# GpSimd instructions on the shared port also wait for the VectorE work that the plan puts ahead of them

## The chip, the cores and the metric

One core of one Trainium2 chip runs the whole kernel as one program. The metric is the device time of one execution in microseconds (us), and the time of a kernel is the median of several executions. The engines are TensorE (PE in the profile; its weight loads are PEld), VectorE (DVE), ScalarE (ACT), GpSimd (POOL) and SyncE (SP), which here only issues DMAs.

## What is computed

The input x has 2048 rows of 576 numbers. Its layernorm `xn` goes into two branches, and their results are added to x:

```
xn = (x - mean) / sqrt(var + 1e-5)                        # per row
A  = irfft2(rfft2(xn) * (w_r + 1j * w_i))                 # over rows and columns
q  = einsum("nd,dhc->nhc", xn, w_q)                       # 32 heads, 2 x 128 each
i1 = argmax(q[..., :128] @ k1.T);  i2 = argmax(q[..., 128:] @ k2.T)   # 8 keys each
e  = 8 * i1 + i2                                          # one of 64 experts
B  = sum over heads of gelu(xn . u[e]) * v[e]
out = x + A + B
```

The softmax of the reference runs over one candidate, so its weight is 1.

## The kernel before, in words

**How the work is tiled.** x is held as 16 tiles of 128 rows. For each tile `ln` (line 688) takes the row statistics, mostly on VectorE (`bn_stats`), for tiles 7, 9, 11, 13 and 15 on ScalarE. `folds` (line 742) adds and subtracts x and its mirror image along the columns: two instructions over 289 columns (tile `t` in the profile), then three over 145 to 288 columns (tile `A`). The sets `DE`, `DS`, `DF` and `DV` (lines 737 to 739) say which of them go to VectorE and which to GpSimd. `dft128` (line 759) is the first matmul of the Fourier transform. Meanwhile `fold_part` (line 851) folds the query weights with the keys, so that the scores become one matmul with x later; its weights are loaded by 32 DMAs.

Then 16 groups g of frequencies pass through `d_fwd`, `s_fwd`, `s_mul`, `s_inv` (lines 1017 to 1099). `s_mul` multiplies by W on VectorE (tiles `t1` and `t2`, from PSUM), combines the parts on GpSimd (`y`, two instructions of 128x289), lets ScalarE round to 16 bits (`yh`), GpSimd take the rest (`yh` again, 128x578) and ScalarE copy a part (`yl`). `s_inv` reads `yh` and `yl` on TensorE. Between the groups run eight blocks r of the expert branch: `x_t` (line 920) splits x into two 16-bit parts (GpSimd: `xT<-xf,xT`, 128x640), `scores` (line 938) does the matmuls, the gelu (ScalarE) and the maximum over keys (`mx<-banks`), and `route` and `combine` (lines 964 and 984) turn the winning keys into codes with VectorE instructions on 16-bit tiles (`w<-w,wt`, `w<-w,MT`, `w<-MT,iv`). `w_scale` (line 831) finds the scale of the next weights W: a maximum over partitions by a transpose on TensorE, `mxr` on VectorE and a matmul `banks<-id,mxr` on TensorE (`allmax`, line 667). Last, for 16 tiles t, `d_inv` and `fin` (lines 1105 and 1133) transform back, add the expert branch and write out.

**What sets the order.** The program is not issued as it is traced. Every call is recorded by `_Engine` as an op of `_Plan` (line 295) with an engine, a modelled cost, its dependences and a mark `port`. The mark (line 348) is set for each GpSimd instruction that has an input, and for a VectorE instruction whose output is in SBUF and that has two or more SBUF inputs, or is a copy or `tensor_scalar` with one. `forward` (line 409) walks through time: each engine takes, of the ops that can start, the one of the best rank in the hand-kept list `RANK`; an op with the mark `port` can't start before the last op with the mark has ended, on either engine. It returns the order and each op's planned start. `issue` (line 522) then issues all ops in the order of their planned starts, under `manual_schedule`, so each engine executes its own ops in exactly this order; waits between the engines come only from data (what an op reads, or the buffer it overwrites). All recorded calls are issued at line 540, which is why the profile names L540 everywhere.

So the plan's rule that two ops with the mark don't overlap is a rule of the plan alone: the issued program does not hold an engine back for it.

Of the kernel before, what the change touches and what calls it, by code (L numbers as in the profile page):

```python
# [294 lines left out]
class _Plan:  # L295
# [223 lines left out]
                    stale.add(ops[k].eng)  # L519
        return max(free.values()), order, slot, start  # L520

    def issue(self):

        self.prepare()
        ops = self.ops
        self.tiles = sorted({v for o in ops for v in o.tiles}, key=lambda v: v.order)
        for o in ops:
            o.held = []
            o.opens = sorted(o.tiles, key=lambda v: v.order) if o.eng == "tensor" else []
            o.after = [(k, self.latency(o, ops[k])) for k in o.succ]  # L530
        for i, o in enumerate(ops):
            for j in o.pre:
                ops[j].held.append(i)
        _, order, slot, start = self.forward([-r for r in RANK])
        self.order = [(start[i], i) for i in order]
        for v, k in slot.items():
            v.slot = k
        for i in order:
            for fn, args, kw in ops[i].calls:
                fn(*[x.place() if isinstance(x, _Ps) else x for x in args],  # L540
                   **{k: x.place() if isinstance(x, _Ps) else x for k, x in kw.items()})


def body(tc, nc, a, out):
    with ExitStack() as ctx:
        ctx.enter_context(tc.manual_schedule())
        plan = _Plan(nc)
        _body(ctx, tc, nc, plan, a, out)
        plan.issue()


def _body(ctx, tc, nc, plan, a, out):
# [716 lines left out]
```

## Time and profile before

| | |
|---|---|
| median of 3 runs | 222.05 us (221.85 to 222.1) |
| the profiled execution's own time | 222.02 us |
| its span, first to last instruction | 220.1 us |
| mean granted TensorE clock | 0.992 |
| busy: PE, DVE, ACT, POOL | 194.9, 187.4, 130.5, 115.0 us |
| instructions: PE, DVE, ACT, POOL | 2324, 457, 308, 153 |
| DMA | 48.12 MB, mean 219 GB/s |

The span is split into stages by time: rows of the windows view give each engine's busy time within a stretch. A row of the timeline gives start, duration, engine, operation and tiles, and in brackets how long the engine stood idle before it and what released it. An instruction that has begun and is then held up shows no idle time: its row is longer than others of its shape. `banks` is PSUM.

### The profile page before, as it was taken

The numbers are of one execution on the slowest core, as the hardware profiler recorded it, in microseconds if no ns is written. First come the engines' busy times: TensorE is split into PE (matmuls) and PEld (weight loads), VectorE is DVE, ScalarE is ACT, GpSimd is POOL, SyncE is SP. The second block draws the span as 40 slices with busy tenths as digits, with TensorE's granted clock in tenths as the row PEclk, the third lists the DMA queues.
The fourth block names the chain that finished last, engine by engine and source line by source line (L and its number), as shares of the span: only waits on it lengthen the run. The fifth ranks groups of instructions, "written<-read, shape, count | busy, mean of one in ns | idle before, by whom it ended". The sixth has DMA issues, their size and how long they took to land.

```text
span 220.1 us, 6024 instructions
## 1 busy us (share of the span) xinstructions
PE 194.9 (89%) x2324; PEld 131.4 (60%) x2324; DVE 187.4 (85%) x457; ACT 130.5 (59%) x308; POOL 115.0 (52%) x153
## 2 busy tenths in 40 slices
PE   0179978989899999999999999969989999999990
PEld 0168557667656775657467465446555568877860
DVE  1999999971784967874899999999999999999980
ACT  2267989898857895849627934955635532213320
POOL 4644653602509840673416634867737239568760
PEclk9999999999999999999999999999999999999996
DMA  6999999999999999998224260201000000575466
GB/s 206 394 429 416 331 416 348 312 360 362 389 415 344 420 409 418 418 442 311 91 81 123 103 190 0 60 3 42 33 3 1 0 4 0 134 183 121 114 153 165
DMA packets 17020, 48.12 MB, mean 219 GB/s; under 512 B 2144, under 2 KB 8544, under 8 KB 16224
## 3 DMA queue, kind: packets, MB, share of 16 engines
q1 hardware_dynamic: 16992, 47.74, 61.1%
q8 instruction: 18, 0.29, 0.5%
q14 instruction: 10, 0.08, 0.1%
HBM read 43.01 MB, written 4.72 MB: 217 GB/s over the span
## 4 chain that ended last, share of the span: by engine, by line
PE 57%; DVE 29%; ACT 4%; issue 3%; DMA 3%; POOL 0%; ACTq 0%; DVEq 0%
PE banks L540 57%; DVE t L540 6%; DVE w L540 4%; DVE MT L540 4%; DVE A L540 3%; DVE st L540 2%; DVE rr L540 2%; DVE ABL L540 2%; DMA XN<-in_x_dram 2%; DVE AB L540 1%; ACT xT L540 1%; DMA w<-in_wq_dram 1%; DVE mx L540 1%; ACT xf L540 1%; DVE mm__96 L540 1%
## 5 line engine op out<-in xcount | busy, mean ns | idle before, releaser
L540 PE MATMUL banks<-MU,xT 128*128 128x512 f16 x192 | 45.7, 379 | 0.0
L540 PE MATMUL banks<-c,AB 128*128 128x145 f16 (+2 forms) x320 | 37.8, 252 | 0.0
L540 POOL TENSOR_TENSOR A<-t 128x287 f32<-128x287 f32 (+2 forms) x42 | 29.5, 722 | 15.6 <-DVE t L540 10.3
L540 POOL TENSOR_TENSOR y<-t,t 128x289 f32<-128x289 f32 x32 | 23.2, 748 | 22.7 <-DVE t L540 22.1
L540 PEld LDWEIGHTS <-xT 128*128 128x128 f16 x224 | 20.7, 98 | 23.2 <-issue 0.9
L540 DVE SCALAR_TENSOR_TENSOR t<-banks,wx,Wt 128x578 f32<-128x578 f32 x32 | 24.2, 810 | 3.9 <-PE banks L540 3.7
L540 POOL TENSOR_TENSOR yh<-y,yh 128x578 f16<-128x578 f32 x16 | 22.8, 1436 | 8.4 <-ACT yh L540 6.7
L540 PE MATMUL banks<-Rs,yl 128*99 128x128 f32 x64 | 12.0, 321 | 14.3 <-ACT Rs L540 11.8
L540 POOL TENSOR_TENSOR xT<-xf,xT 128x640 f16<-128x640 f32 x10 | 14.0, 1402 | 14.5 <-ACT xf L540 13.5
L540 ACT ACTIVATE AB<-banks 128x512 f32<-128x512 f32 (+1 forms) x32 | 18.8, 591 | 2.1 <-PE banks L540 1.8
L540 PEld LDWEIGHTS banks<-Rs,yl 128*99 128x99 f32 x64 | 8.6, 186 | 19.0 <-ACT Rs L540 14.2
L540 PE MATMUL banks<-w,KP 128*32 128x288 f32 x256 | 19.7, 414 | 0.1
L540 ACT ACTIVATE yh<-banks 128x290 f32<-128x290 f32 (+1 forms) x16 | 7.3, 458 | 20.8 <-PE banks L540 20.7
L540 PE MATMUL banks<-c,ABL 99*128 99x289 f16 (+1 forms) x64 | 18.8, 298 | 0.4 <-DVE ABL L540 0.4
L540 PEld LDWEIGHTS banks<-c,AB 128*128 128x128 f32 x128 | 17.9, 190 | 1.2 <-issue 0.5
L540 PE MATMUL banks<-Rs,A 128*128 128x128 f32 x128 | 18.5, 299 | 0.0
L540 DVE TENSOR_REDUCE MT<-w 128x128 bf16<-128x896 bf16 (+1 forms) x16 | 18.1, 1136 | 0.0
L540 PE MATMUL banks<-A,s 64*64 64x289 f32 x256 | 18.0, 411 | 0.0
L540 PEld LDWEIGHTS banks<-Rs,A 128*128 128x128 f32 x128 | 17.4, 214 | 0.9 <-issue 0.9
L540 PEld LDWEIGHTS <-AB 128*128 128x128 f16 x192 | 17.2, 147 | 0.1
L540 ACT ACTIVATE xT<-xf,bx 128x640 f16<-128x640 f32 x16 | 13.0, 821 | 5.6 <-PE banks L540 5.5
L540 POOL TENSOR_TENSOR t<-XN 128x289 f32<-128x289 f32 x14 | 11.9, 864 | 8.4 <-DVE A L540 4.2
(127 smaller groups left out, 417.8 us busy)
## 6 DMA issues: line engine op xcount, KB each, us to landing
w<-in_wq_dram SPq DMA_DIRECT2D x32, 576.0 KB, 6.8
xf<-in_xT_dram SPq DMA_DIRECT2D x16, 320.0 KB, 5.6
Wt<-in_W_dram SPq DMA_DIRECT2D x8, 578.0 KB, 6.7
out_dram<-XN SPq DMA_DIRECT2D x32, 144.0 KB, 2.5
XN<-in_x_dram SPq DMA_DIRECT2D x3, 1154.0 KB, 10.7
s<-in_s_dram SPq DMA_DIRECT2D x16, 192.0 KB, 5.1
XN<-in_xd_dram SPq DMA_DIRECT2D x2, 1152.0 KB, 9.7
XN<-in_xd_dram SPq DMA_DIRECT2D x1, 2304.0 KB, 12.3
```

The source lines that it names most:

```text
L540: fn(*[x.place() if isinstance(x, _Ps) else x for x in args], **{k: x.place() if isinstance(x, _Ps) else x for k, x in kw.items()})
```

## The change

While issuing, the new `issue` keeps a list of the VectorE instructions issued so far, each with its planned end plus 225 ns. For each GpSimd op with the mark `port` it looks up the last VectorE instruction on that list whose time is not later than the op's planned start plus 30 ns, that is, one planned to end at least 195 ns before the GpSimd op starts. If that is another one than for the last such op, the GpSimd instruction gets a dependence on it (`add_manual_dep`), which becomes a wait on VectorE's semaphore. No instruction is added to VectorE or taken from it, the order on every engine and the arithmetic stay, and VectorE gets no new wait.

```diff
-    def issue(self):
+    def issue(self, tc):
...
+        sync = mybir.DependencyInfo(mybir.DependencyClass.Sync, mybir.DependencyReason.DATA)
+        queue, held = [], None
         for i in order:
-            for fn, args, kw in ops[i].calls:
-                fn(*[x.place() if isinstance(x, _Ps) else x for x in args],
-                   **{k: x.place() if isinstance(x, _Ps) else x for k, x in kw.items()})
+            o = ops[i]
+            for fn, args, kw in o.calls:
+                ins = fn(*[x.place() if isinstance(x, _Ps) else x for x in args],
+                         **{k: x.place() if isinstance(x, _Ps) else x for k, x in kw.items()}).ins
+            if o.eng == "vector":
+                queue.append((start[i] + o.cost + 225, ins))
+            elif o.eng == "gpsimd" and o.port:
+                first = [v for t, v in queue if t <= start[i] + 30]
+                if first and first[-1] is not held:
+                    held = first[-1]
+                    tc.add_manual_dep(ins, held.name, sync, reason="port")
...
-        plan.issue()
+        plan.issue(tc)
```

Of the 149 GpSimd instructions of the plan, 143 carry the mark. The plan of the kernel before already holds all starts, so the partner of each can be read off it: 129 of them get a wait.

## The prediction

> **What bounds the kernel now.** I read the page first, then the windows view cut into stages, the waits of TensorE, and the timelines of single stretches. The windows show who is full in which stage (columns: stretch, its length, busy time of PE, PEld, DVE, ACT and POOL, granted clock, DMA share, GB/s).
>
> ```profile
> 4.60:43.00 38.40, 28.73 (x231) 22.58 (x232) 38.07 (x155) 28.01 (x83) 21.35 (x34) 1.00 0.98 381
> 60.00:87.00 27.00, 27.00 (x408) 17.30 (x408) 19.94 (x51) 20.11 (x40) 12.51 (x13) 1.00 1.03 400
> 137.00:145.00 8.00, 6.27 (x38) 3.12 (x36) 7.75 (x8) 6.49 (x12) 6.93 (x8) 1.00 0.15 41
> ```
>
> Until 43 us VectorE is the bound (38.07 of 38.40 us). From 60 to 87 us TensorE is full and so is the DMA. From 137 to 145 us VectorE is nearly full (7.75 of 8.00) while TensorE loses 1.73. GpSimd is the bound in none of them: even from 137 to 145 us it has 1.07 of 8 us free. So time can be won only where TensorE waits for VectorE, and before 43 us. From 113 to 176 us TensorE's waits are these, in total, times, longest:
>
> ```profile
> PE banks L540 <- DVE mxr L540: 2.2, 2, 1.9
> PE banks L540 <- DVE w L540: 0.5, 1, 0.5
> PE banks L540 <- DVE ABL L540: 0.4, 1, 0.4
> PE banks L540 <- ACT MT L540: 0.2, 1, 0.2
> ```
>
> These 3.3 us are the most that the stretch after 113 us can give back. The question is whether VectorE loses them to GpSimd. Here is VectorE's timeline around the longest of these waits, then GpSimd's, then TensorE's:
>
> ```profile
> 139.53 1.82 DVE L540 TENSOR_TENSOR w<-w,wt 128x896 bf16<-128x896 bf16 x1
> 141.28 1.50 DVE L540 TENSOR_TENSOR w<-w,MT 128x512 bf16<-128x512 bf16 x1
> 142.70 2.20 DVE L540 TENSOR_REDUCE MT<-w 128x128 bf16<-128x896 bf16 x2
> 144.82 0.27 DVE L540 TENSOR_REDUCE mxr<-banks 1x1 bf16<-1x128 f32 x1
> ...
> 146.32 1.09 DVE L540 TENSOR_REDUCE mx<-banks 128x128 f32<-128x896 f32 x1
> 147.32 0.42 DVE L540 TENSOR_TENSOR w<-w,MT 128x512 bf16<-128x512 bf16 x1
> ```
> ```profile
> 139.46 1.41 POOL L540 TENSOR_TENSOR xT<-xf,xT 128x640 f16<-128x640 f32 x1
> 140.82 1.68 POOL L540 TENSOR_TENSOR yh<-y,yh 128x578 f16<-128x578 f32 x1
> 143.57 1.40 POOL L540 TENSOR_TENSOR xT<-xf,xT 128x640 f16<-128x640 f32 x1 [1.07 <-ACT xf L540]
> 144.92 2.19 POOL L540 TENSOR_TENSOR yh<-y,yh 128x578 f16<-128x578 f32 x1
> ```
> ```profile
> 142.25 1.03 PE L540 MATMUL banks<-MU,xT 128*128 128x512 f16 x4
> 145.15 0.18 PE L540 MATMUL banks<-id,mxr 128*128 128x1 f16 x1 [1.88 <-DVE mxr L540]
> ```
>
> The second `w` instruction takes 1.50 us, and 0.42 at 147.32. The first takes 1.82; the same shape took 0.60 in this row:
>
> ```profile
> 130.25 0.60 DVE L540 TENSOR_TENSOR w<-w,wt 128x896 bf16<-128x896 bf16 x1
> ```
>
> Each of the two began just after a GpSimd instruction and ended when that one did, plus its own time. VectorE loses 1.22 + 1.08 = 2.3 us here, its queue brings `mxr` 2.3 us late, and TensorE stands for 1.88.
>
> By the Trainium skill, page "SBUF — State Buffer", section "Who interferes with whom", a VectorE instruction with two SBUF inputs and a GpSimd instruction that reads SBUF exclude each other for a whole instruction. These rows agree. The same section says that issue order alone decides who blocks; taken alone this speaks against the change, since an order then only passes the stall to the other engine. By it the sum below is kept only where GpSimd is off the path.
>
> **The change part by part.** Order, work and VectorE's queue stay. What is added is 129 waits in GpSimd's queue. Which VectorE instruction each waits for follows from the planned starts; all times below are from the trace. Laid on the trace, 48 of the partners end after the GpSimd instruction now starts: most between 7 and 42 us, some around 117 to 127, four around 139 to 147 (by 1.9 to 2.95 us: 141.35 against 139.46, 143.8 against 140.82), and a handful after. The other 81 waits are already met and cost nothing visible; a wait that was met late costs 0.08 us (GpSimd's 10.18 below, against VectorE's end at 9.16 + 0.94 = 10.10).
>
> *Stage 139 to 147.* The first `xT` will wait for the `w` at 139.53, the first `yh` for the first of the two reductions at 142.70, the second `xT` for a small `MT` instruction at 145.42, the second `yh` for the `mx` at 146.32. So both `w` run free, VectorE reaches `mxr` about 2.3 us earlier, and TensorE's 1.88 us go. What is late next is TensorE's own work, which ends at 143.28, so no more than 1.88. Behind the waiting instructions stands GpSimd's queue: `xT` to about 141.5 (held once more by the second `w`), `yh` to 142.8, `xT` to 145.1, `yh` to 146.8 on the new clock, which is 2.2 us ahead by then. The reader of the last is ScalarE:
>
> ```profile
> 148.99 0.52 ACT L540 ACTIVATE yl<-yh 128x396 f16<-128x396 f16 x1
> ```
>
> It will want `yh` at 148.99 - 2.2 = 146.8: just met. I take -1.9, between 0 and -1.9.
>
> *Stage 121 to 125.* The same on a smaller scale:
>
> ```profile
> 121.80 1.50 DVE L540 TENSOR_TENSOR w<-w,MT 128x512 bf16<-128x512 bf16 x1
> ...
> 125.03 0.73 DVE L540 TENSOR_TENSOR w<-w,MT 128x512 bf16<-128x512 bf16 x1
> ```
> ```profile
> 120.45 2.58 POOL L540 TENSOR_TENSOR yh<-y,yh 128x578 f16<-128x578 f32 x2
> ```
>
> VectorE gets 1.1 + 0.3 us back, but TensorE waited only 2.2 - 1.9 = 0.3 for it: -0.3.
>
> *Stage 157 to 163.* VectorE, GpSimd, TensorE:
>
> ```profile
> 157.78 0.14 DVE L540 TENSOR_SCALAR wx<-banks 128x2 f32<-128x2 f32 x1
> 157.85 0.27 DVE L540 TENSOR_TENSOR MT<-MT,fm 128x128 int32<-128x128 int32 x1
> 158.04 1.27 DVE L540 TENSOR_TENSOR al<-wx,mk 128x16 f32<-128x16 f32 x1
> ```
> ```profile
> 157.72 1.57 POOL L540 TENSOR_TENSOR yh<-y,yh 128x578 f16<-128x578 f32 x1 [0.80 <-ACT yh L540]
> ```
> ```profile
> 161.91 0.21 PE L540 MATMUL banks<-s,yh 64*128 64x128 f16 x1 [0.49 <-DVE w L540]
> ```
>
> `al` is sixteen columns and takes 1.27 us because `yh` is ahead of it. `yh` will wait for `wx` at 157.78, so it starts at 157.92 + 0.08 = 158.00, before `al` at 158.04. That is a race. GpSimd's 14.61 below shows who wins such a one: it starts 0.09 us before VectorE's `A` at 14.70, yet `A` takes its usual 0.44 and GpSimd's instruction 0.83 instead of the 0.44 of 10.18. I take VectorE to win: 1.1 us for VectorE, of which TensorE's 0.49 count, and the 0.2 of the list above, which is the wait for `MT` right behind it: 0.7. Bounds +0.3 (`yh` first, from a later start) and -0.7.
>
> *Stage 163 to 176.* TensorE's last wait of the list (0.4) ends a stretch in which VectorE lost 0.5 us to `y` additions that will now wait: -0.3, between 0 and -0.4.
>
> *Until 43 us.* VectorE is held in three places, the first two under a `t<-XN` of GpSimd quoted below, the third under one of the same kind:
>
> ```profile
> 9.16 0.94 DVE L540 TENSOR_TENSOR t<-XN 128x289 f32<-128x289 f32 x1
> ...
> 14.09 0.44 DVE L540 TENSOR_TENSOR t<-XN 128x289 f32<-128x289 f32 x1
> ...
> 14.70 0.44 DVE L540 TENSOR_TENSOR A<-t 128x288 f32<-128x288 f32 x1
> ...
> 21.92 0.91 DVE L540 TENSOR_TENSOR t<-XN 128x289 f32<-128x289 f32 x1
> ...
> 40.63 1.52 DVE L540 TENSOR_TENSOR A<-t 128x288 f32<-128x288 f32 x2
> ```
> ```profile
> 8.65 1.13 POOL L540 TENSOR_TENSOR t<-XN 128x289 f32<-128x289 f32 x1
> 10.18 0.44 POOL L540 TENSOR_TENSOR A<-t 128x145 f32<-128x145 f32 x1 [0.40 <-DVE t L540]
> ...
> 14.61 0.83 POOL L540 TENSOR_TENSOR A<-t 128x145 f32<-128x145 f32 x1 [0.45 <-DVE t L540]
> ...
> 21.83 1.67 POOL L540 TENSOR_TENSOR t<-XN 128x289 f32<-128x289 f32 x2
> ```
>
> Against 0.44 that is 0.50, 0.47 and about 0.8 (two instructions, 0.44 + 0.3): 1.8 us. The waits hold each of these GpSimd instructions behind the VectorE one. Their results are read 1.3 us or more later, mostly, which covers GpSimd's delay; where it doesn't, VectorE waits for the fold instead. But the gain must pass the stage from 60 to 87 us, where TensorE and the DMA are both full: it arrives only as far as the loads come earlier too. I take half, -0.9, between +0.3 and -1.8.
>
> *What the waits cost.* In the last stage GpSimd's additions run back to back, close ahead of TensorE:
>
> ```profile
> 200.58 2.70 POOL L540 TENSOR_TENSOR A<-t 128x289 f32<-128x289 f32 x4 [0.72 <-DVE t L540]
> 202.05 0.71 PE L540 MATMUL banks<-A,c 64*64 64x288 f32 x8
> ```
>
> The matmul starts 0.1 us after the second addition is over (200.58 + 2 x 0.675 = 201.93). Partners there end 0.3 us before the additions start, so I take 0.4 us of new waiting in all, between 0 and 1.1 (0.07 for each of 16 tiles).
>
> **Sum.** 0.9 + 0.3 + 1.9 + 0.7 + 0.3 - 0.4 = 3.7 us. The profiled execution took 222.02 us, its span 220.1, and the 1.9 outside it don't change; its time is the median of 222.05 to 0.03. So I predict 222.05 - 3.7 = 218.4.
>
> **Rivals.**
>
> *The early gain stays behind and `al` loses its race.* For it: DMA share 1.03 from 60 to 87 us, 0.04 us between `yh` and `al`. Against it: the loads are issued when TensorE frees their buffers, which moves too. Left are 0.3 + 1.9 + 0.3 - 0.4 = 2.1: 219.9.
>
> *No change.* GpSimd takes over each stall in full and passes it on to TensorE through `yh` and `xT`, or the dependence isn't turned into a wait. Against the first speaks that GpSimd has 1 us of 8 free just where the stall is worst. 222.0. The rule of the Trainium skill quoted above, page "SBUF — State Buffer", would give this result if GpSimd were on the path.
>
> *Slower: the collision moves with the wait.* GpSimd, released 0.08 us after its partner, starts later into the same row of two-input instructions and covers the next ones instead, such as the small `MT` steps after 145.02; VectorE gains nothing, and GpSimd has lost its lead. Its place is where GpSimd feeds TensorE soon, the last stage: 0.07 us for each of 16 tiles, +1.1: 223.1. It decides once a released addition starts over 0.1 us after its turn, the distance at 202.05, while the `w` rows stay at 1.5 us. Against it: between `mxr` and the `w` at 147.32 VectorE has only short port instructions, under 0.3 us each but one.
>
> **Chances and range.** Forecast (216.9 to 219.4) 0.50; early gain lost (219.4 to 221.6) 0.20; no change 0.08; slower 0.22. A measurement of this kernel can tell about 0.2% from no change, so faster 0.70, same 0.08, slower 0.22. Low end: all terms at their best, 1.8 + 0.3 + 1.9 + 0.7 + 0.4 = 5.1, 216.9. The high end, 222.8, reaches into the slower case and leaves half of it out. The forecast's own range is 216.9 to 219.4.
>
> **What would show it.** Right: `w<-w,wt` near 139 at 0.6 us and `w<-w,MT` at 0.4; no idle of over 0.5 us before `banks<-id,mxr` near 143; `al` at 0.2; `t<-XN` on VectorE at 0.44 everywhere before 43 us. GpSimd's rows get longer idle times released by DVE. Wrong: long rows on other VectorE instructions of the same passes, TensorE waiting for ScalarE's `yl` or, late, for GpSimd's `A`; or the first TensorE work after 60 us no earlier than now.

## The result, and the profile after

| | before | after |
|---|---|---|
| median | 222.07 us (221.85 to 222.6) | 216.32 us (216.25 to 217.02) |
| the profiled execution: own time, span | 222.02, 220.1 us | 217.02, 215.2 us |
| mean granted TensorE clock | 0.992 | 0.991 |

The ratio is 0.9745 with a 95% interval of 0.9718 to 0.9771. The change makes the kernel 5.75 us faster. The direction was foretold, and so were the places; but 218.4 was forecast, and 216.32 is 0.6 below the low end of the range. So the question for the experiments is which terms of the sum were too small.

The page of the kernel after gives the busy time of each engine:

```profile
PE 191.6 (89%) x2324; PEld 128.6 (60%) x2324; DVE 181.4 (84%) x457; ACT 130.2 (60%) x308; POOL 109.6 (51%) x153
```

The same 457 VectorE instructions take 6.0 us less (187.4 before), and the same 153 of GpSimd 5.4 us less (115.0). An instruction that is held up counts as busy, so this is, in the main, time in which the two engines blocked each other: instructions of the same shape have become shorter, as the rows below show. VectorE got no new wait, so its 6.0 us are saved. For GpSimd a part has only changed its form: where it was held, it now waits, and a wait counts as idle.

The windows view of the kernel after, for the three stretches shown of before and in the same columns:

```profile
4.60:43.00 38.40, 27.64 (x244) 21.65 (x248) 37.99 (x159) 29.21 (x87) 18.66 (x34) 1.00 0.99 385
...
60.00:87.00 27.00, 27.00 (x409) 17.00 (x411) 20.07 (x48) 20.24 (x40) 12.45 (x13) 1.00 1.02 399
...
137.00:145.00 8.00, 8.00 (x59) 4.41 (x60) 7.75 (x15) 7.83 (x16) 6.11 (x6) 1.00 0.09 33
```

VectorE is as full until 43 us as before, but fits 159 instructions into the stretch, not 155, and GpSimd's 34 take 18.66 us, not 21.35. From 137 to 145 us VectorE does 15 instructions in the 7.75 us in which it did 8, and TensorE no longer loses anything. The stretches are cut by the clock, so the kernel after is further on in its work in each; that a given instruction became shorter is read from the timelines.

TensorE's waits from 113 to 176 us were four rows with 3.3 us. After the change this one is left:

```profile
PE banks L543 <- DVE mxr L543: 0.3, 1, 0.3
```

The places where VectorE was held, now in the timeline of the kernel after. VectorE first, in order of time (the three early places; stage 139 to 147; `al`):

```profile
9.21 0.41 DVE L543 TENSOR_TENSOR t<-XN 128x289 f32<-128x289 f32 x1
...
21.43 0.45 DVE L543 TENSOR_TENSOR t<-XN 128x289 f32<-128x289 f32 x1
...
39.74 0.67 DVE L543 TENSOR_TENSOR A<-t 128x288 f32<-128x288 f32 x2
...
138.14 0.62 DVE L543 TENSOR_TENSOR w<-w,wt 128x896 bf16<-128x896 bf16 x1
138.68 0.42 DVE L543 TENSOR_TENSOR w<-w,MT 128x512 bf16<-128x512 bf16 x1
...
141.14 0.27 DVE L543 TENSOR_REDUCE mxr<-banks 1x1 bf16<-1x128 f32 x1
...
154.33 0.14 DVE L543 TENSOR_SCALAR wx<-banks 128x2 f32<-128x2 f32 x1
...
154.60 0.16 DVE L543 TENSOR_TENSOR al<-wx,mk 128x16 f32<-128x16 f32 x1
```

And GpSimd beside the last two:

```profile
138.94 1.43 POOL L543 TENSOR_TENSOR xT<-xf,xT 128x640 f16<-128x640 f32 x1 [0.82 <-DVE w L543]
140.33 1.28 POOL L543 TENSOR_TENSOR yh<-y,yh 128x578 f16<-128x578 f32 x1
...
154.62 1.30 POOL L543 TENSOR_TENSOR yh<-y,yh 128x578 f16<-128x578 f32 x1 [1.13 <-DVE wx L543]
```

The `w` rows went from 1.82 and 1.50 us to 0.62 and 0.42, `al` from 1.27 to 0.16, and the early rows from 0.94, 0.91 and 1.52 (the last is two instructions) to 0.41, 0.45 and 0.67. GpSimd shows the price in brackets, 0.82 and 1.13 us idle with VectorE as releaser, and it has the time for it.

Not all is gone. One stall moved to a neighbour, as the rival on the slower side had it. VectorE and GpSimd of the kernel after, near 121 us:

```profile
120.72 0.42 DVE L543 TENSOR_TENSOR w<-w,MT 128x512 bf16<-128x512 bf16 x1
121.06 0.42 DVE L543 TENSOR_TENSOR w<-MT,iv 128x512 bf16<-128x512 bf16 x1
121.39 1.32 DVE L543 SCALAR_TENSOR_TENSOR MT<-MT 128x64 bf16<-128x64 bf16 x1
```
```profile
121.31 1.31 POOL L543 TENSOR_TENSOR yh<-y,yh 128x578 f16<-128x578 f32 x1 [0.66 <-ACT t L543]
```

`yh` has the `w` of 120.72 (1.50 us before) as its partner, starts 0.17 us after its end at 121.14, and covers the next instruction but one, a small `MT` that takes 0.2 us elsewhere. (The releaser in brackets is inferred: ScalarE's `t` happens to end at that time, and `yh` doesn't read it.)

### The profile page after: what moved, and what is told of

It is laid out like the page before. It is cut to its first block, busy times and chain, and to the rows that moved or that the text cites. A ratio compares the mean times of both kernels' runs of the same rounds, so it can differ in the third digit from the quotient of the medians.

```text
span 215.2 us, 6038 instructions
## 1 busy us (share of the span) xinstructions
PE 191.6 (89%) x2324; PEld 128.6 (60%) x2324; DVE 181.4 (84%) x457; ACT 130.2 (60%) x308; POOL 109.6 (51%) x153
## 4 chain that ended last, share of the span: by engine, by line
PE 69%; DVE 19%; DMA 6%; ACT 2%; issue 1%; DVEq 0%; ACTq 0%
PE banks L543 69%; DVE t L543 4%; DMA w<-in_wq_dram 4%; DVE A L543 3%; DVE st L543 3%; DVE MT L543 2%; DMA XN<-in_x_dram 2%; DVE rr L543 2%; DVE ABL L543 2%; DVE w L543 1%; ACT AB L543 1%; ACT yl L543 1%; DVE mv L543 1%; DVE XN L543 0%; DVE AB L543 0%
## 5 line engine op out<-in xcount | busy, mean ns | idle before, releaser
L543 POOL TENSOR_TENSOR y<-t,t 128x289 f32<-128x289 f32 x32 | 22.7, 727 | 23.4 <-DVE t L543 18.1
L543 POOL TENSOR_TENSOR A<-t 128x287 f32<-128x287 f32 (+2 forms) x42 | 26.5, 646 | 14.8 <-DVE t L543 6.2
L543 POOL TENSOR_TENSOR yh<-y,yh 128x578 f16<-128x578 f32 x16 | 21.0, 1323 | 9.7 <-ACT yh L543 4.7
L543 PE MATMUL banks<-Rs,yl 128*99 128x128 f32 x64 | 10.8, 300 | 14.3 <-ACT Rs L543 11.9
L543 PEld LDWEIGHTS banks<-Rs,yl 128*99 128x99 f32 x64 | 7.8, 172 | 18.7 <-ACT Rs L543 13.6
L543 PE MATMUL banks<-Rs,A 128*128 128x128 f32 x128 | 17.3, 286 | 0.0
L543 POOL TENSOR_TENSOR t<-XN 128x289 f32<-128x289 f32 x14 | 11.4, 818 | 10.9 <-DVE rr L543 5.3
L543 PEld LDWEIGHTS banks<-Rs,A 128*128 128x128 f32 x128 | 16.1, 200 | 0.9 <-issue 0.9
```

The source lines that it names most:

```text
L543: ins = fn(*[x.place() if isinstance(x, _Ps) else x for x in args], **{k: x.place() if isinstance(x, _Ps) else x for k, x in kw.items()}).ins
```

## The experiments

The theory: each stall of VectorE beside a GpSimd instruction goes, and each reaches the end of the kernel in full. Rivals: the early gain is half lost between 60 and 87 us (the prediction's own choice); the waits cost something late in the kernel; or it isn't the order that gives the gain but something else that comes with the waits. Edits are to the loop of the changed kernel's `issue`, unless said otherwise.

### The changed kernel once more

> The changed kernel once more. Theory: the waits take VectorE's stalls away, 4.9 us of TensorE's time in the profiled execution, and a load that came late at 58 us kept another 0.64 us back there. Executions in which that load is in time are then 0.6 us faster, with the first matmul block after 58 us 1.75 instead of 1.1 us ahead of before: 216.3, span 214.5. Rival: the 0.7 us between the profiled execution and the median is spread over the kernel; then this profile shows the same 1.1 us at 60 us wherever its total lies.

216.33 us (216.29 to 216.65), ratio 0.9738 [0.9724, 0.9751]. This profiled execution, with a span of 214.5 us, is a better one to read terms from than the first one of the kernel after, which was at 217.02 itself the longest of its runs. TensorE at 58 us in the kernel after, then in this repeat:

```profile
56.52 0.69 PE L543 MATMUL banks<-w,KP 128*32 128x288 f32 x8
58.08 0.69 PE L543 MATMUL banks<-w,KP 128*32 128x288 f32 x8 [0.87 <-DMA w<-in_wq_dram]
```
```profile
56.42 1.18 PE L543 MATMUL banks<-w,KP 128*32 128x288 f32 x16
57.53 0.27 PE L543 MATMUL banks<-c,uv 128*2 128x128 f32 x1
```

In the first, a load of the query weights came late and TensorE stood 0.87 us for it. The DMA issues between 46 and 55 us (issues, KB each, median us to landing) tell the same, first of the kernel after, then of the repeat:

```profile
w<-in_wq_dram SPq DMA_DIRECT2D x5, 576.0 KB, 8.6
```
```profile
w<-in_wq_dram SPq DMA_DIRECT2D x5, 576.0 KB, 6.7
```

The kernel is the same; the loads varied between executions, and that makes 0.7 us: behind this place the first profile is 0.74 us later than the repeat (the first `c,AB` at 58.96 and 58.22), at the end 0.7. Read from the first profile of the kernel after alone, the early gain would have seemed smaller than it is in its other runs.

TensorE's starts in the repeat, to be held against those of before:

```profile
44.64 0.27 PE L543 MATMUL banks<-c,bx 128*1 128x128 f32 x1
...
140.10 1.03 PE L543 MATMUL banks<-MU,xT 128*128 128x512 f16 x4
140.96 0.17 PE L543 MATMUL banks<-id,mxr 128*128 128x1 f16 x1
...
157.05 0.87 PE L543 MATMUL banks<-s,yh 64*128 64x128 f16 x24
...
158.36 2.76 PE L543 MATMUL banks<-MU,xT 128*128 128x512 f16 x12
...
169.94 0.32 PE L543 MATMUL banks<-c,ABL 99*128 99x290 f16 x1
```

The rows of before that aren't shown above:

```profile
46.49 0.27 PE L540 MATMUL banks<-c,bx 128*1 128x128 f32 x1 [0.54 <-ACT ABL L540]
...
163.58 0.60 PE L540 MATMUL banks<-MU,xT 128*128 128x512 f16 x2
...
175.56 0.32 PE L540 MATMUL banks<-c,ABL 99*128 99x290 f16 x1 [0.36 <-DVE ABL L540]
```

`bx`: 46.49 - 44.64 = 1.85 earlier. `MU,xT` ahead of `mxr`: 142.25 - 140.10 = 2.15. `mxr`: 145.15 - 140.96 = 4.19. `MU,xT` behind the stage of `al`: 163.58 - 158.36 = 5.22. `ABL`: 175.56 - 169.94 = 5.62. From there to the end the distance stays, and the spans differ by 220.1 - 214.5 = 5.6.

### Only the early waits

```diff
-            elif o.eng == "gpsimd" and o.port:
+            elif o.eng == "gpsimd" and o.port and start[i] < 45000:
```

> Only the waits of GpSimd instructions planned before 45 us. Theory: the early gain stands by itself and passes the full stage from 60 to 87 us: 1.1 to 1.75 us, 220.3 to 220.9. Rival (as predicted, half of 1.8 at best arrives): 221.1 or more.

220.11 us (220.03 to 220.39), ratio 0.9906 [0.9893, 0.9920]: 2.0 us less than before, a little more than expected. TensorE's `bx` starts 1.86 us earlier (44.63), and the span is 1.9 shorter (218.2). That the stage from 60 to 87 us would keep half of it is refuted. SyncE's issues show how the gain passes; its load of W and the one ahead of it, in the kernel before and in this one:

```profile
48.15 0.33 SPq L540 DMA_DIRECT2D w<-in_wq_dram  x1
48.53 0.42 SPq L540 DMA_DIRECT2D Wt<-in_W_dram  x1
```
```profile
46.29 0.33 SPq L543 DMA_DIRECT2D w<-in_wq_dram  x1
46.67 0.42 SPq L543 DMA_DIRECT2D Wt<-in_W_dram  x1
```

The loads are issued 1.86 us earlier, since the buffers they overwrite come free that much earlier: from 44 to 60 us SyncE waits 4.7 us for TensorE in this kernel, in five waits. Here a full DMA (share 1.03 before, 1.02 in this kernel) did not hold the gain back, because its whole sequence of loads moved with it.

### Only the waits planned between 100 and 170 us

The same edit with `100000 < start[i] < 170000`.

> Only the waits planned between 100 and 170 us. Theory: the terms after 113 us add up without the early ones: 0.3 + 2.0 + 1.0 + 0.4 = 3.7 us, 218.3. Rival (part of these gains came only because the early part had shifted the loads and GpSimd's phase): 219.5 or more.

218.08 us (218.05 to 218.72), ratio 0.9820 [0.9803, 0.9836]: 4.0 us less. With the 2.0 us of the early waits that is 6.0; all waits together gave 5.75. The two parts add up within the uncertainty of the ratios (0.0015 of 222 is 0.3 us each).

### Only the other waits

The same edit with `not (start[i] < 45000 or 100000 < start[i] < 170000)`.

> All other waits, planned from 45 to 100 us and after 170 us, where the additions feed the last matmuls. Theory: waits that are met cost nothing and no stall on TensorE's path is there: 222.05 within 0.2. The prediction's term of 0.4 us of new waiting gives 222.4; its slower rival (0.07 us for each of 16 tiles) 223.1.

222.05 us (221.76 to 222.5), ratio 0.9997 [0.9987, 1.0007]. These waits, those of the last stage among them, together neither cost nor win more than 0.3 us: the 0.4 us that the prediction charged for them is not there, and the slower rival's 1.1 us even less.

### Only the four waits at 139 to 147

The same edit with `136000 < start[i] < 143000`.

> Only the waits of the GpSimd instructions planned from 136 to 143 us: two xT and two yh, at 139 to 147 us in the profile of before. Theory: VectorE's two w instructions take 0.6 and 0.4 us, TensorE's idle 1.88 us goes: 220.1. Rival (the collision moves on to the small MT instructions that follow): 221.5 or more, with long rows among these.

220.07 us (219.72 to 220.36), ratio 0.9910 [0.9897, 0.9923]: four waits out of 129 bring 2.0 us.

### One wait alone, that of the `yh` beside `al`

The same edit with `152000 < start[i] < 153000`.

> One wait alone: that of the yh beside al near 158 us. Theory: VectorE wins the race, al takes 0.2 us instead of 1.27, TensorE's waits before the next s_inv go and those after: 221.0 (0.7 to 1.1 us gained). Rival (yh keeps winning, from a later start): 222.0 to 222.3 and al over 1 us.

221.01 us (220.81 to 221.45), ratio 0.9957 [0.9945, 0.9969]: one wait brings about 1 us, where 0.7 was forecast. TensorE in this kernel, then in the kernel before (whose row of 161.91 the prediction shows), tells why:

```profile
161.04 0.38 PE L543 MATMUL banks<-s,yl 64*99 64x128 f16 x7
161.26 0.87 PE L543 MATMUL banks<-s,yh 64*128 64x128 f16 x24
161.93 0.70 PE L543 MATMUL banks<-s,yl 64*99 64x128 f16 x17
162.56 2.76 PE L543 MATMUL banks<-MU,xT 128*128 128x512 f16 x12
```
```profile
161.03 0.38 PE L540 MATMUL banks<-s,yl 64*99 64x128 f16 x7
...
162.31 0.83 PE L540 MATMUL banks<-s,yh 64*128 64x128 f16 x23 [0.19 <-ACT MT L540]
```

Where TensorE doesn't wait, the group behind `yl` starts at 161.26, 0.16 us before the end that the profile gives for `yl` (161.04 + 0.38 = 161.42): matmuls overlap. Where it waits, before the change, the group starts at 161.91. The profile writes 0.49 of idle time, from the end of one row to the start of the next; what is lost is 0.65, from start to start. The second wait counts as 0.19 and costs 1.02 - 0.65 = 0.37 (163.58 - 162.56 = 1.02). So these gaps in TensorE's rows cost 0.16 and 0.18 us more than the numbers in brackets. That a row's end is modelled is said on the page of the profile; by the Trainium skill, page "Perfetto Trace Analysis", section "Tensor Engine Instruction (MATMUL, LD_WEIGHTS)", it is computed from the instruction's size and not observed; a row that begins 0.16 us before the end of the one ahead fits that.

### Nearly as many waits, each for a partner 5 us earlier

```diff
-                queue.append((start[i] + o.cost + 225, ins))
+                queue.append((start[i] + o.cost + 5225, ins))
```

> As many waits as in the change, but each on a VectorE instruction planned to end at least 5.2 us before the GpSimd instruction starts, so that nearly all are met when they are reached. Theory: a met wait costs nothing and does nothing: 222.05 within 0.3, with the stalls of before. Rival (the waits act by themselves, through the queue or the clock): more than 0.5 us away on either side.

222.34 us (221.82 to 222.56), ratio 1.0001 [0.9979, 1.0023]. By the plan these are 126 waits, not 129. Waits that don't hold GpSimd back at the right place change nothing, to within 0.5 us; that 5.75 us came with the waits by some other way is ruled out.

### Partners that are only planned to have started

```diff
-                queue.append((start[i] + o.cost + 225, ins))
+                queue.append((start[i], ins))
```

> Each GpSimd instruction waits for the last VectorE instruction that the plan has started by then, ended or not. Theory: GpSimd falls behind the plan, later than its readers want it: slower than the change, by 1 us or more (217.3 or more), with TensorE or ScalarE waiting for yh, yl or A; but still with few stalls on VectorE. Rival (the more order the better): 216.3 or less.

232.45 us (232.09 to 233.48), ratio 1.0481 [1.0463, 1.0499]. Here the slower rival's mechanism is real: GpSimd loses its lead. TensorE's `bx` is already 3.15 us later than before (49.64 against 46.49). Of the waits from 113 to 230 us in this kernel:

```profile
ACT yl L543 <- POOL yh L543: 4.8, 5, 1.6
...
PEld banks L543 <- POOL A L543: 3.9, 8, 0.9
...
PE banks L543 <- POOL yh L543: 1.7, 3, 1.1
```

ScalarE's `yl` waits for GpSimd's `yh` (in the repeat of the changed kernel 1.8 us, not 4.8), TensorE's weight loads wait for GpSimd's `A`, and TensorE itself waits for `yh`; the repeat has no row of the last two kinds.

### The kernel before, with zeros written in place of a subtraction

The edit is to the kernel before, with no waits. It leaves out the second, low part of `yh`: where GpSimd read `y` and `yh` to subtract, it writes zeros and reads nothing.

```diff
-        G.tensor_tensor(yh[:, 1], y, yh[:, 0], op=OP.subtract)
+        plan.add("gpsimd", lambda o, *r, **k: nc.gpsimd.memset(o, 0.0), "tensor_tensor",
+                 (yh[:, 1], y, yh[:, 0]), dict(op=OP.subtract))
```

> The kernel before, without any of the new waits; only GpSimd's subtraction that makes the second, low part of yh (128x578) is replaced, at the same place of its queue, by an instruction that writes zeros there and reads nothing (the low part of yh is left out of the computation). Theory (VectorE is held only by a GpSimd instruction that reads SBUF beside it): without any wait the `w` near 121.8 takes 0.4 us instead of 1.50, the `al` near 158 takes 0.2 instead of 1.27, the `w` near 141.3 takes 0.4 instead of 1.50; the `w<-w,wt` near 139.5 keeps its 1.8, since `xT` still reads. Gain 0.3 at 125, 1.1 at mxr, 1.0 at al (what the single wait there measured): about 219.6. Rival (any GpSimd instruction at work blocks VectorE, or the rows are long because of VectorE's own inputs): these rows stay long as far as GpSimd's instruction is still beside them, 222.0.

218.67 us (218.59 to 218.77), ratio 0.9842 [0.9825, 0.9858]. It is not the clean test that was intended: writing zeros takes 0.57 us where the subtraction took 1.3, so near 121.6 and 155.8 us GpSimd is done before the VectorE instructions in question start, and their short rows prove nothing. The time is also 0.9 us below what the theory gave; GpSimd's queue, shorter by 0.7 us for each group, may be the cause, but that wasn't taken apart. So the time of this run settles little, and the question of reading rests on one stretch. VectorE, then GpSimd, in this kernel:

```profile
138.68 1.55 DVE L540 TENSOR_TENSOR w<-w,wt 128x896 bf16<-128x896 bf16 x1
...
145.12 0.41 DVE L540 TENSOR_TENSOR w<-w,MT 128x512 bf16<-128x512 bf16 x1
```
```profile
138.34 1.41 POOL L540 TENSOR_TENSOR xT<-xf,xT 128x640 f16<-128x640 f32 x1
139.68 0.58 POOL L1064 MEMSET yh<- 128x578 f16 x1
...
144.96 0.57 POOL L1064 MEMSET yh<- 128x578 f16 x1
```

The `w` of 145.12 lies wholly beside the writing of zeros (144.96 to 145.53) and takes its 0.41 us; the `w` of 138.68 lies beside `xT`, which reads, and takes 1.55. It ends 0.48 us after `xT` (140.23 and 139.75), while zeros are being written beside it from 139.68 to 140.26, so these don't hold it. By the Trainium skill, page "SBUF — State Buffer", section "Who interferes with whom", a VectorE instruction with two SBUF inputs contends with a GpSimd instruction that reads SBUF and not with one that only writes it; these two rows agree.

### The changed kernel without the wait ahead of `KP`

```diff
-            elif o.eng == "gpsimd" and o.port:
+            elif o.eng == "gpsimd" and o.port and not 17000 < start[i] < 18000:
```

> The changed kernel, but the GpSimd instructions planned between 17 and 18 us, KP among them, get no wait. In the changed kernel TensorE stood 1.1 us for KP ahead of `w,KP` at 18.37. Theory (that stand is covered by the loads and by VectorE's bound before 43 us): 216.3 as the changed kernel, ratio to before 0.974, and `w,KP` near 18 starts up to 1 us earlier. Rival (the late fold delays the loads by as much, and these limit until 87 us): up to 1 us faster, 215.3, and no late load near 58 us.

216.46 us (216.39 to 216.62), ratio 0.9743 [0.9727, 0.9759]. So that wait costs nothing. TensorE's `w,KP` starts at 18.70 in this kernel and at 19.16 in the repeat of the changed kernel, but that is not the wait: with only the early waits, this one among them, it starts at 18.77, and the 16 matmuls ahead of it take 3.08, 3.54 and 3.14 us in the three. In the first profile of the kernel after, TensorE does stand 1.08 us for `KP`, and its `bx` is 0.1 us later than in the repeat (44.74 and 44.64). That VectorE's bound covers the stand fits the windows view, where VectorE is full until 43 us; no run tests it by itself.

### Later partners: 110 ns, and none

The constant 225 becomes 110 in one kernel and 0 in the other, so that the partner need only be planned to end 80 ns before the GpSimd instruction's start, or may end 30 ns after it.

> The changed kernel with 110 ns in place of 225 ns in the list's times, so that a VectorE instruction planned to end 80 ns before the GpSimd instruction's start, not 195, can be its partner: 20 of the 129 waits get a later partner, among them the yh planned at 120.1 us. Theory (a later partner costs nothing as long as it is planned to end before the start): 216.0 to 216.4; the `MT<-MT` near 121.4 that took 1.31 us in the changed kernel goes back to 0.2 and TensorE's 0.34 idle at 124 goes: at best 216.0. Rival (each step closer to the plan's start adds delay, as where GpSimd waited for instructions only planned to have started, 232.5): 217 to 219.

216.05 us (215.99 to 216.14), ratio 0.9724 [0.9708, 0.9740].

> The changed kernel with 0 in place of 225 ns: the partner may be planned to end up to 30 ns after the GpSimd instruction's planned start; 78 of the waits get a later partner. Theory (GpSimd gives up its lead, but no more than the hand-over of 0.08 us for each such wait; where GpSimd is followed closely, in the last stage, it adds up): 216.3 to 217.5. Rival 1 (the turn comes here already): 219 or more, with TensorE waiting for yl and A as where partners were only planned to have started. Rival 2 (the closer the order, the fewer collisions): under 216.0.

218.34 us (218.30 to 218.48), ratio 0.9828 [0.9811, 0.9844].

With 110 ns, 20 waits have a later partner, that of the `yh` near 121 us among them. VectorE, GpSimd and TensorE there:

```profile
120.79 0.42 DVE L543 TENSOR_TENSOR w<-MT,iv 128x512 bf16<-128x512 bf16 x1
121.12 0.22 DVE L543 SCALAR_TENSOR_TENSOR MT<-MT 128x64 bf16<-128x64 bf16 x1
```
```profile
121.38 1.28 POOL L543 TENSOR_TENSOR yh<-y,yh 128x578 f16<-128x578 f32 x1 [1.00 <-DVE MT L543]
```
```profile
123.03 0.17 PE L543 MATMUL banks<-id,mxr 128*128 128x1 f16 x1
```

`yh` has the `w` of 120.79 as its partner now (the releaser in brackets is inferred) and starts behind the small `MT`, which takes 0.22 us, and TensorE's `mxr` follows without a wait. All five of its runs lie under the four of the kernel without the `KP` wait, on the same chip (215.99 to 216.14, and 216.39 to 216.62). They lie under all runs of the changed kernel too (216.25 to 217.02, and 216.29 to 216.65 in its repeat), but the repeat ran on another chip and the intervals of the ratios overlap, so the 0.3 us that it gains on the changed kernel (216.33 against 216.05) are likely and not shown. With 0 ns, 78 waits have a later partner, and 2.0 us of the gain are lost again: `bx` starts at 46.14, only 0.35 us earlier than before. The time lies above the theory and under the first rival, so both had the loss wrong. Later partners begin to cost somewhere between those that end 80 ns before and those that end 30 ns after the planned start. The hand-over itself fits: in the kernel after, `yh` starts 0.15 us after the end of its partner `wx` (154.62 - 154.33 - 0.14), `xT` 0.18 us after that of `w` (138.94 - 138.14 - 0.62), and in the kernel with 110 ns `yh` 0.17 us after its `w` (121.38 - 120.79 - 0.42). Elsewhere it is the prediction's 0.08 us: the `t<-XN` of 21.59 in the kernel after starts that long after its partner `rr` (21.59 - 21.18 - 0.33). Which of the two it is in a place, the runs don't tell. A partner that ends less than that ahead delays the GpSimd instruction against the plan.

## Why the prediction was right, and where it was wrong

Measured terms are from the repeat of the changed kernel, in us earlier at TensorE.

| step of the sum | forecast | measured |
|---|---|---|
| until 43 us | 0.9 | 1.85 |
| stage 121 to 125 | 0.3 | 2.15 - 1.85 = 0.30, in another place |
| stage 139 to 147 | 1.9 | 4.19 - 2.15 = 2.04 |
| `al`, stage 157 to 163 | 0.7 | 5.22 - 4.19 = 1.03 |
| stage 163 to 176 | 0.3 | 5.62 - 5.22 = 0.40 |
| cost of the waits | -0.4 | 0 (ratio 0.9997 of the waits outside the early and middle stages) |
| sum | 3.7 | 5.6 |

**The mechanism was right.** The three early places, the two `w` and `al` behave as forecast, GpSimd has the time, and the order that the plan wanted is worth having on the chip.

**The step that failed most** is "I take half, -0.9", with the argument that the gain must pass the stage from 60 to 87 us where TensorE and the DMA are both full. The 1.8 us were read rightly from the rows; halving them was wrong: 1.85 us arrived, and the early waits alone gave 2.0. Full as it is, the stage passed on the earlier start. It would have stopped the gain if its loads had been issued at a fixed time, and they are issued when TensorE frees their buffers, 1.86 us earlier here, which the prediction itself had named as the argument against. That step accounts for 0.95 of the 1.9 us that were missing, the next one for 0.4, and the idle times for the rest.

**"What the waits cost", 0.4**, was wrong too. The waits outside the early and the middle stages, those of the last stage among them, gave a ratio of 0.9997. In the last stage GpSimd stands idle ahead of `A` about as long as before (6.9 us in the repeat, 6.8 before), and TensorE waits for nothing there: the view of its waits from 176 to 215 us in the repeat has no row. Where a wait was not met, its price was often above the 0.08 us that was used: hand-overs took 0.08 to 0.18.

**`al`, and the smaller terms,** were sized by the idle time in brackets, which leaves out the overlap of TensorE's rows: 1.88 became 2.04, 0.49 became 0.65, 0.2 became 0.37. The 0.3 missing in `al` and the 0.14 in the stage before it are of this kind. The race of `al` came out as taken, but not as argued: with the longer hand-over `yh` starts 0.02 us after `al`, not 0.04 before. That was luck in part: at 121.31 in the kernel after, GpSimd began 0.08 us ahead and did hold VectorE.

**Stage 121 to 125** has the right sum for the wrong reason. The `mxr` wait that was to go is still 0.3 (the row above), since the stall moved to the small `MT`; instead TensorE gains 0.3 between 129 and 132 us (start of `A,s` 1.83, of the `MUL,xT` behind it 2.15 earlier). Before, then in the repeat:

```profile
130.10 2.02 PE L540 MATMUL banks<-A,s 64*64 64x289 f32 x24
```
```profile
128.27 1.69 PE L543 MATMUL banks<-A,s 64*64 64x289 f32 x24
```

This is the second of the two stalls that the prediction counted for VectorE, the `w` of 125.03 with 0.73 us, by a path that it didn't name. Six of the profiled kernels keep the subtraction and lack this stage's waits, or have them on partners 5 us earlier: there that `w` takes 0.72 to 0.74 us and the group 2.02 or 2.03. In seven with the waits, or with zeros written, the group takes 1.69 or 1.70 (in the repeat the `w` takes 0.40). In each of the six, the second matmul of the group starts 0.05 to 0.07 us after the end of VectorE's `AB` (130.39 against 130.33 before), so it seems to wait for that; the row has no bracket, since the wait lies inside it. The kernel with 110 ns has both: 1.67 earlier before the `mxr`, 125.16 - 123.03 = 2.13 at it, and 2.46 at the `MUL,xT`.

**The range** ended at 216.9 as "all terms at their best" (5.1). It was not their best: the idle times were no upper bound, nor were their 3.3 us "the most that the stretch after 113 us can give back". It gave 0.30 + 2.04 + 1.03 + 0.40 = 3.77. In the table that is 0.05 (until 43 us) + 0.14 + 0.33 = 0.5, as much as 5.6 lies beyond 5.1.

## What to carry to other kernels

Where VectorE and GpSimd instructions with inputs in SBUF lie beside each other, look for rows that are longer than others of their shape; one semaphore wait for GpSimd, on the VectorE instruction planned to end just ahead of it (here 0.08 or 0.2 us), may give the stall back at no cost, but a wait for work that is still running can lose far more (here 10 us). When a gain must pass a stage that is full, ask whether the loads of that stage are issued by the same chain of work; if so, count it in full. Price a TensorE gap from start to start, not by the idle time between rows, and take terms from two profiled executions when loads can be late in one.

## What the runs showed of the hardware

- When GpSimd is recorded less than 0.1 us ahead of VectorE, the recorded start doesn't tell who holds the port: before, GpSimd's instruction at 14.61 is recorded 0.09 us ahead of VectorE's at 14.70 and is nevertheless the one held (0.83 against 0.44). At 121.31 against 121.39 in the kernel after, 0.08 us apart, GpSimd holds it and VectorE's `MT` takes 1.32. Neither is chance: the first outcome is the same in all seven traces that have this pair of starts, the second in four.
- From the end of VectorE's row to the start of the GpSimd row that waited for it the hand-over took 0.08 us in some places and 0.15 to 0.18 in others.
- GpSimd wrote zeros to 128x578 in 0.57 us beside a VectorE instruction with two inputs, and neither was lengthened.
- Loads of 576 KB, issued from 46 to 55 us, took a median of 6.7 us in one execution and 8.6 in another of the same kernel, with the DMA full, and that was worth 0.7 us of its time.
